# Planned issue and landing times of the small transfers of attention probabilities, in a kernel of attention and two MoE layers

## The chip, the core and the metric

The kernel runs on one core of a Trainium2 chip. The metric is device time in microseconds (us), the median of three runs. The engines named below are PE (TensorE, matrix products), DVE (VectorE), ACT (ScalarE), POOL (GpSimd) and SP (SyncE, which here issues nearly all DMA transfers, one after the other). Each engine takes its instructions in the order in which the program lists them.

## What is computed

Attention of 4 batches, 8 heads, 576 positions and 64 values per head, half of the heads with a local mask and half with a strided one; then a dense layer with squared ReLU; then a layer of 8 experts of which each token takes one.

```python
scores = scale * np.matmul(q, k.transpose(0, 1, 3, 2))
mask_local = (rel >= 0) & (rel < 32)
mask_strided = (rel >= 0) & (pos[None, :] % 32 == pos[:, None] % 32)
attn = softmax(np.where(masks, scores, -1e9))
x = np.matmul(attn, v)                      # to (2304 tokens, 512)
h = x @ w_in                                # 512 x 2048, the first layer
g = s * np.maximum(h, 0.0) ** 2 + b
x1 = g @ w_out                              # 2048 x 512, the second layer
out[mask_e] = gate * (np.maximum(x1[mask_e] @ w1[e], 0.0) @ w2[e])   # e of 8 experts
```

## The kernel before

The 2304 tokens are cut into five units (256, 512, 512, 512 and 512 tokens). Attention is cut into 23 groups, 0 to 22. The first nine take a transposing path on PE; groups 9 to 22 (the late groups, `attn_late`, line 780) are spread over the time in which PE does the dense layer of earlier units, and this is where the change lies.

The dense layer is a row of steps, one for each unit and each block of 128 hidden columns: `h` is computed by the first layer (line 1039, twelve matrix products of up to 512 columns), ACT and DVE make `g` of it (lines 987 to 1013), and the second layer (line 1073, again twelve) adds `g` times a weight block to four banks. A product of `float32r` halves is made of three passes, hence twelve.

A late group goes through these stages. Line 575 loads its queries and keys, and in another load its values. Line 800 makes the scores on PE into two banks. DVE adds the mask (line 815), takes maxima, subtracts, ACT takes the exponential (823), DVE sums and scales (825 to 830) and transposes blocks of 32 by 32 into `prt` (834). Line 842 moves the 32-row pieces of `prt` to their places in `phs`: eight small transfers of 32 KB for most groups, four for groups 13 and 18, all issued by SP. Line 857 then multiplies with the values on PE; this text calls it the product of the group. ACT and DVE split the result into a high and a low part in `xsl` (875, 879), which the first layer of the unit reads.

`prt`, `phs`, and the buffers of late queries/keys and of late values exist once each. So the transfers of a group wait for the product of the group before it, and so does the load of a group's values. The scores take a pair of banks, the product one bank of that pair.

The order of all this is not written by hand. `Order.run` (line 280) is a planner that runs while the program is built: each piece of work is a generator that yields `op((engine, duration), waits=...)`, and the planner always issues next what, by its own clocks, can start first. `("DMA", d)` occupies one clock of the planner's that stands for SP's queue, shared by all loads and transfers. `o.fin` is the planned end of the piece, `DMA_LAT` (1.8) what the planner adds until data have landed, and `t1` the planned landing of the small transfers: from then on the product may be placed (`ev`), and `prt` used again (`t_pt`). The durations in the planner do not bind the chip; they decide only in which order instructions stand on each engine.

Of the kernel before, what the change touches and what calls it, by code (L numbers as in the profile page):

```python
# [122 lines left out]
def span(g):  # L123
    kind, b, i0, n = GROUPS[g]
    if kind == "L":
        return b * S + i0 * QB, b * S + (i0 + n) * QB
    j0, j1, _ = part_of(g)
    return b * S + j0 * STRIDE, b * S + j1 * STRIDE
# [60 lines left out]
DMA_LAT = 1.8  # L189
# [114 lines left out]
def op(*engs, waits=(), dep=True, on=(), late=0.0):  # L304
    return engs, waits, dep, on, late
# [6 lines left out]
def body(ctx, tc, qkv, w12, moe_s, moe_b, wg, e12, out):  # L312
# [64 lines left out]
    o = Order()  # L377
# [68 lines left out]
    t_qe, t_qk, t_vv, t_pt, t_ph = Tok(NQE), Tok(1), Tok(1), Tok(1), Tok(1)  # L446
# [109 lines left out]
    for g, (kind, b, i0, n) in enumerate(GROUPS):  # L556
        t0, t1 = span(g)
# [23 lines left out]
    def attn(g):  # L581
        kind, b, i0, n = GROUPS[g]
        strided = kind == "P"
        if g >= NEARLY:
            yield from attn_late(g)
            return
# [193 lines left out]
    def attn_late(g):  # L780
# [51 lines left out]
        nb = 2 if w > QG else 1  # L832
# [1 line left out]
        nc.vector.transpose(out=prt[:, 0:nb * m * QG].rearrange("p (b c q) -> p b c q", b=nb, q=QG),  # L834
                            in_=pr[:, 0:m * 2 * QG].rearrange("p (c b q) -> p b c q", b=2, q=QG)[:, 0:nb])
        o.free(t_p)
        yield op(("DMA", 0.4 * nb), waits=[t_ph])
        for x in range(2):
            for y in range(nb):
                for p in range(2):  # L840
                    a, r = p * QB + x * QG, x * QB + y * QG
                    nc.sync.dma_start(out=phs[r:r + QG, p, x, 0:m * QG], in_=prt[a:a + QG, y * m * QG:(y + 1) * m * QG])
        t1 = o.fin + DMA_LAT
        o.free(t_pt, t1)
        ev = Ev()
        o.set(ev, t1)
# [1224 lines left out]
```

## Time and profile before

| what | value |
|---|---|
| median of 3 runs | 699.63 us (699.41 to 704.1) |
| the profiled execution, own time | 702.58 us |
| span of its first to last instruction | 700.8 us |
| PE busy | 674.9 us, 96% of the span |
| DVE busy | 345.7 us, 49% |
| ACT busy | 284.9 us, 41% |
| POOL busy | 39.5 us, 6% |
| share of 16 DMA engines' span taken by SP's queue | 29.4% |

A profile row names the line, the engine, the operation and the tiles (out<-in). In the timeline a row holds equal instructions that follow each other without a gap: start, length, count, and in brackets how long the engine had been idle before and what ended that. SPq is SP's queue: the time there is that of issuing, not of moving the data. Matrix products are pipelined, so a row's length ends after the start of the next one; the distance between the starts of two rows is what the first cost.

### The profile page before, as it was taken

The page shows a single profiled execution, that of the slowest core. Times are in us where ns is not written, and L with a number is a line of the kernel's source. Part 1 is how long each engine was busy: PE and PEld are TensorE (multiplying, and loading weights), DVE is VectorE, ACT ScalarE, POOL GpSimd, SP SyncE. Part 2 cuts the span into 40 slices and gives each one's busy share as a digit, 9 for nine tenths or more (in the row PEclk, how much of TensorE's full clock was granted, in tenths as well). Part 3 has the DMA queues.
Part 4 walks back from the last instruction along what each step waited for, and adds up shares of the span by engine and source line. Part 5 has one row for each costly group of instructions (what it writes and reads, how often), then busy time and mean ns, then how long its engine had stood idle before and what let it go on. Part 6 is the DMA issues. An engine that isn't in the chain of part 4 may idle for free. (4 is left out here: it accounts for less than half of the span.)

```text
span 700.8 us, 12794 instructions
## 1 busy us (share of the span) xinstructions
PE 674.9 (96%) x5028; PEld 568.6 (81%) x5028; DVE 345.7 (49%) x809; ACT 284.9 (41%) x598; POOL 39.5 (6%) x140
## 2 busy tenths in 40 slices
PE   8899999898998999999999999999999999999996
PEld 7788878797776778867877878888899899998896
DVE  6898886662253222134331134444567854764340
ACT  5777454454352233343333364554431432424221
POOL 7640000000000000000000000001000000000000
PEclk9999999999999999999999999999999999999999
DMA  8975156232323102031211023110120262307101
GB/s 314 406 272 173 55 172 215 69 117 81 115 98 118 58 24 65 1 134 52 72 36 46 1 90 121 61 61 31 61 91 1 71 230 99 121 1 256 64 12 63
DMA packets 31089, 72.32 MB, mean 103 GB/s; under 512 B 5806, under 2 KB 11695, under 8 KB 30259
## 3 DMA queue, kind: packets, MB, share of 16 engines
q1 hardware_dynamic: 30898, 71.46, 29.4%
q8 instruction: 40, 0.66, 0.4%
q14 instruction: 23, 0.18, 0.1%
q0 software_dynamic: 128, 0.02, 0.0%
HBM read 56.77 MB, written 11.69 MB: 98 GB/s over the span
## 5 line engine op out<-in xcount | busy, mean ns | idle before, releaser
L1039 PE MATMUL h<-xsl,w 128*128 128x512 f32 (+1 forms) x876 | 207.3, 382 | 0.0
L1073 PE MATMUL bk<-g,w 128*128 128x512 f32 (+1 forms) x864 | 198.8, 378 | 0.0
L1039 PEld LDWEIGHTS h<-xsl,w 128*128 128x128 f32 x876 | 157.2, 189 | 31.5 <-issue 0.8
L1073 PEld LDWEIGHTS bk<-g,w 128*128 128x128 f32 x864 | 155.4, 189 | 32.2 <-issue 1.3
L1013 DVE TENSOR_TENSOR g<-r,g 128x512 fp32r<-128x512 f32 (+1 forms) x73 | 48.1, 659 | 156.1 <-ACT g L1011 155.9
L987 ACT ACTIVATE r<-h 128x512 f32<-128x512 f32 (+1 forms) x80 | 44.4, 556 | 194.4 <-PE h L1039 190.6
L1544 PE MATMUL bk<-w,ht 128*128 128x512 f32 x384 | 96.8, 393 | 0.0
L1544 PEld LDWEIGHTS bk<-w,ht 128*128 128x128 f32 x384 | 68.6, 188 | 12.2
L1011 ACT ACTIVATE g<-r 128x512 fp32r<-128x512 f32 (+1 forms) x73 | 44.2, 605 | 2.7
L999 ACT ACTIVATE r<-r 128x512 f32<-128x512 f32 (+1 forms) x73 | 44.2, 606 | 2.2
L1437 ACT ACTIVATE ht<-h 128x256 fp32r<-128x256 f32 x24 | 9.2, 385 | 74.6 <-PE h L1598 54.8
L857 PE MATMUL bk<-phs,qkv 128*64 128x64 f32 (+2 forms) x408 | 17.9, 232 | 15.3 <-DMA phs<-prt 12.3
L857 PEld LDWEIGHTS bk<-phs,qkv 128*64 128x64 f32 x408 | 15.1, 143 | 21.4 <-issue 18.0
L1598 PEld LDWEIGHTS h<-x,wa 128*128 128x128 f32 x192 | 26.4, 188 | 2.4 <-issue 0.4
L1598 PE MATMUL h<-x,wa 128*128 128x256 f32 x192 | 28.0, 281 | 0.0
L1598 PE MATMUL bk<-x,wc 128*128 128x256 f32 x192 | 27.8, 280 | 0.0
L1598 PE MATMUL h<-x,wc 128*128 128x256 f32 x192 | 27.7, 280 | 0.0
L1598 PEld LDWEIGHTS h<-x,wc 128*128 128x128 f32 x192 | 25.6, 188 | 1.3 <-DVE su L1475 0.3
L879 DVE TENSOR_TENSOR xsl<-bk,xsl 128x512 fp32r<-128x512 f32 (+4 forms) x14 | 8.6, 613 | 35.5 <-ACT xsl L875 35.5
L875 ACT ACTIVATE xsl<-bk 128x512 fp32r<-128x512 f32 (+4 forms) x14 | 7.5, 535 | 43.1 <-PE bk L857 43.0
L1598 PEld LDWEIGHTS bk<-x,wc 128*128 128x128 f32 x192 | 24.8, 188 | 0.2 <-issue 0.2
L815 DVE TENSOR_TENSOR pr<-bk,ml 128x288 f32<-128x288 f32 (+5 forms) x17 | 7.6, 462 | 26.2 <-PE bk L800 26.2
(245 smaller groups left out, 748.1 us busy)
## 6 DMA issues: line engine op xcount, KB each, us to landing
raw<-w SPq DMA_DIRECT2D x32, 512.0 KB, 7.8
qkv<-qkv SPq DMA_DIRECT2D x14, 512.0 KB, 4.0
qkv<-qkv SPq DMA_DIRECT2D x8, 544.0 KB, 3.7
out<-ob SPq DMA_DIRECT2D x17, 256.0 KB, 3.2
xd<-x SPq DMA_DIRECT2D x4, 1024.0 KB, 3.8
wraw<-e SPq DMA_DIRECT2D x16, 256.0 KB, 2.7
xr<-xd SPq DMA_DIRECT2D x8, 512.0 KB, 5.2
X<-xd SPq DMA_DIRECT2D x4, 1024.0 KB, 10.1
```

What stands on the lines that cost most here:

```text
L815: nc.vector.tensor_tensor(out=ps4[:, :, i:j], in0=sc[:, :, i:j], in1=mask.unsqueeze(1).unsqueeze(1).to_broadcast([P, 2, j - i, w]), op=ALU ...
L857: nc.tensor.matmul(out=og[h * D:(h + 1) * D, p * tot + 2 * i * nq:p * tot + 2 * (i + 1) * nq], lhsT=vv[:, i, p, h, :], rhs=phs[:, p, :, c: ...
L879: nc.vector.tensor_sub(out=dst[1], in0=src, in1=dst[0].bitcast(F32))
L987: nc.scalar.activation(out=r, in_=h, func=AF.Relu)
L999: nc.scalar.activation(out=to, in_=r, func=AF.Square)
L1011: nc.scalar.activation(out=gt[:, 0, 0:U], in_=r, func=AF.Copy)
L1013: nc.vector.tensor_sub(out=gt[:, 1, 0:U], in0=r, in1=gt[:, 0, 0:U].bitcast(F32))
L1039: nc.tensor.matmul(out=h, lhsT=w_t[2 * fc][:, a, c * P:(c + 1) * P], rhs=xt(u, c, x), start=(c == 0 and n == 0), stop=(c == KD - 1 and n = ...
L1073: nc.tensor.matmul(out=acc[pu][c], lhsT=w_t[2 * pf + 1][:, a, c * P:(c + 1) * P], rhs=gt[:, x, 0:cols(pu)], start=(first and n == 0), stop ...
L1437: nc.scalar.activation(out=ht[:, 0, a:b], in_=src, func=AF.Relu)
L1544: nc.tensor.matmul(out=acc2[s, t][0], lhsT=box[k][:, x, t * P:(t + 1) * P], rhs=w_t["p", 2 * f + 1][:, a, :], start=(f == 0 and n == 0), s ...
L1598: nc.tensor.matmul(out=banks[to], lhsT=t[:, a, off + c * P:off + (c + 1) * P], rhs=x2[s, b][:, y, c, :], start=(first and c == 0 and n == ...
```

## The change

Two numbers in `attn_late` are changed: what the planner counts for issuing the small transfers, and what it adds until they have landed. `nb` is 2 for eight transfers and 1 for four.

```diff
-        yield op(("DMA", 0.4 * nb), waits=[t_ph])
+        yield op(("DMA", 2.55 * nb), waits=[t_ph])
         for x in range(2):
             for y in range(nb):
                 for p in range(2):
                     a, r = p * QB + x * QG, x * QB + y * QG
                     nc.sync.dma_start(out=phs[r:r + QG, p, x, 0:m * QG], in_=prt[a:a + QG, y * m * QG:(y + 1) * m * QG])
-        t1 = o.fin + DMA_LAT
+        t1 = o.fin + DMA_LAT + 0.4
```

For eight transfers the planner now counts 5.1 for the issue where it counted 0.8, and 2.2 until landing where it counted 1.8. No instruction is added or dropped on PE, SP and POOL; one eviction of 64 columns goes from ACT to DVE. What differs is the order.

On PE, in the middle of unit 3, the place of the product of group 20 (`bk_3659` before, `bk_3821` now), with the scores of group 21 (`bk_3795` before, `bk_3775` now). Before:

```order
L1039 MATMUL h<-xsl,w 128x512 x6
L857 MATMUL bk_3659<-phs,qkv 64x64 x16
L1039 MATMUL h<-xsl,w 128x512 x6
L1073 MATMUL bk_930<-g,w 128x512 x3
L1073 MATMUL bk_931<-g,w 128x512 x3
L1073 MATMUL bk_932<-g,w 128x512 x3
L1073 MATMUL bk_933<-g,w 128x512 x3
L1039 MATMUL h<-xsl,w 128x512 x6
L800 MATMUL bk_3795<-qkv 32x36 x32
L1039 MATMUL h<-xsl,w 128x512 x6
```

And now, from the same twelve matrix products of line 1039 on:

```order
L1039 MATMUL h<-xsl,w 128x512 x12
L1073 MATMUL bk_930<-g,w 128x512 x3
L1073 MATMUL bk_931<-g,w 128x512 x3
L1073 MATMUL bk_932<-g,w 128x512 x3
L1073 MATMUL bk_933<-g,w 128x512 x3
L1039 MATMUL h<-xsl,w 128x512 x6
L800 MATMUL bk_3775<-qkv 32x36 x32
L1039 MATMUL h<-xsl,w 128x512 x6
L857 MATMUL bk_3821<-phs,qkv 64x64 x16
```

The product moved behind 30 matrix products of the dense layer and behind the scores of group 21, which were after it.

On PE, in unit 2, the products of groups 14 and 15. Before, from the product of group 14 to that of group 15:

```order
L857 MATMUL bk_2684<-phs,qkv 64x64 x16
L1204 MATMUL bk_2683<-pick,lts 128x16 x4
L1073 MATMUL bk_932<-g,w 128x512 x3
L1073 MATMUL bk_933<-g,w 128x512 x3
L1039 MATMUL h<-xsl,w 128x512 x12
L1073 MATMUL bk_930<-g,w 128x512 x3
L1073 MATMUL bk_931<-g,w 128x512 x3
L1073 MATMUL bk_932<-g,w 128x512 x3
L1073 MATMUL bk_933<-g,w 128x512 x3
L857 MATMUL bk_2683<-phs,qkv 64x64 x16
```

And now, again from the product of group 14 (`bk_2694`) to that of group 15 (`bk_2695`):

```order
L857 MATMUL bk_2694<-phs,qkv 64x64 x16
L1073 MATMUL bk_930<-g,w 128x512 x3
L1073 MATMUL bk_931<-g,w 128x512 x3
L1073 MATMUL bk_932<-g,w 128x512 x3
L1073 MATMUL bk_933<-g,w 128x512 x3
L1039 MATMUL h<-xsl,w 128x512 x12
L1073 MATMUL bk_930<-g,w 128x512 x3
L1073 MATMUL bk_931<-g,w 128x512 x3
L1073 MATMUL bk_932<-g,w 128x512 x3
L1073 MATMUL bk_933<-g,w 128x512 x3
L857 MATMUL bk_2695<-phs,qkv 64x64 x16
```

Both products moved back, and 36 matrix products of the dense layer stand between them where 30 and the small products of line 1204 stood.

On SP, at the same place: `xd_76` is the store of unit 1's result; then come the small transfers of groups 14 and 15, and loads of line 575. The first two loads of 1024 columns are the values of groups 15 and 16, the two of 1032 the queries and keys of groups 16 and 17. Before:

```order
L1169 DMA xd_76<-x_2457 128x2048
L842 DMA phs<-prt 32x256 x8
L575 DMA qkv<-qkv 128x1024
L575 DMA qkv<-qkv 128x1032
L842 DMA phs<-prt 32x256 x8
L575 DMA qkv<-qkv 128x1024
L575 DMA qkv<-qkv 128x1032
L842 DMA phs<-prt 32x256 x8
```

And now:

```order
L1169 DMA xd_76<-x_2468 128x2048
L842 DMA phs<-prt 32x256 x16
L575 DMA qkv<-qkv 128x1024
L575 DMA qkv<-qkv 128x1032
L575 DMA qkv<-qkv 128x1024
L575 DMA qkv<-qkv 128x1032
L842 DMA phs<-prt 32x256 x8
```

The eight transfers of group 15 moved ahead of the values of group 15, directly behind those of group 14.

## Rows read from the trace of the kernel before

**Rows 1.** Busy time by engine in two stretches: from:to length, then busy us (instructions) per engine, PEclk, DMA share, GB/s.

```profile
90.00:130.00 40.00, 38.68 (x348) 31.25 (x346) 31.05 (x63) 17.94 (x33) 0.13 (x2) 1.00 0.51 166
...
380.00:700.00 320.00, 315.27 (x1864) 274.03 (x1863) 154.16 (x413) 114.89 (x214) 5.09 (x16) 1.00 0.23 79
```

**Rows 2.** Waits of PE: engine, line waited for: us in total, times, longest.

```profile
PE bk L857 <- DMA phs<-prt: 12.3, 17, 2.2
...
PE bk L857 <- DMA qkv<-qkv: 2.3, 1, 2.3
...
PE bk L857 <- DVE w L910: 0.3, 1, 0.3
PE bk L857 <- issue: 0.2, 1, 0.2
```

**Rows 3.** Timeline of PE, products of groups 9, 11, 12, 13 and 15.

```profile
96.53 0.76 PE L800 MATMUL bk<-qkv 64*32 64x36 f32 x64
97.23 1.67 PE L1039 MATMUL h<-xsl,w 128*128 128x512 f32 x6
99.23 0.34 PE L857 MATMUL bk<-phs,qkv 128*64 128x64 f32 x4 [0.33 <-DVE w L910]
...
131.25 2.29 PE L857 MATMUL bk<-phs,qkv 128*64 128x48 f32 x32 [1.98 <-DMA phs<-prt]
...
160.32 1.15 PE L857 MATMUL bk<-phs,qkv 128*64 128x64 f32 x32
...
166.81 0.69 PE L857 MATMUL bk<-phs,qkv 128*64 128x64 f32 x16 [2.30 <-DMA qkv<-qkv]
...
218.39 0.34 PE L857 MATMUL bk<-phs,qkv 128*64 128x64 f32 x4 [2.16 <-DMA phs<-prt]
219.02 1.04 PE L857 MATMUL bk<-phs,qkv 128*64 128x64 f32 x28 [0.29 <-DMA phs<-prt]
219.98 4.61 PE L1039 MATMUL h<-xsl,w 128*128 128x512 f32 x12
```

**Rows 4.** Timeline of SP's queue, small transfers and the loads behind them.

```profile
105.67 4.95 SPq L842 DMA_DIRECT2D phs<-prt  x8
...
161.38 2.41 SPq L842 DMA_DIRECT2D phs<-prt  x4
163.83 4.02 SPq L575 DMA_DIRECT2D qkv<-qkv  x3
...
212.58 4.94 SPq L842 DMA_DIRECT2D phs<-prt  x8
```

**Rows 5.** All small transfers of line 842: ns of one min/median/max, and issue to landing.

```profile
L842 SPq DMA_DIRECT2D phs<-prt x104: 507/588/1377, 93.4 to 371.4; - x104
...
DMA to landing us min/median/max: 1.7/1.8/3.8
```

**Rows 6.** Timeline of PE, twelve matrix products of 512 and of 256 columns.

```profile
142.43 1.62 PE L1073 MATMUL bk<-g,w 128*128 128x258 f32 x12
143.88 1.59 PE L1039 MATMUL h<-xsl,w 128*128 128x256 f32 x12
...
344.20 2.88 PE L1039 MATMUL h<-xsl,w 128*128 128x512 f32 x12
346.92 2.88 PE L1073 MATMUL bk<-g,w 128*128 128x512 f32 x12
```

**Rows 7.** DMA issues: loads of line 575, count, KB each, us to landing (208.2:214, then whole span).

```profile
qkv<-qkv SPq DMA_DIRECT2D x1, 512.0 KB, 3.5
...
qkv<-qkv SPq DMA_DIRECT2D x4, 384.0 KB, 9.8
```

**Rows 8.** Busy time as in rows 1, behind the waits of groups 11 and 15.

```profile
131.30:134.70 3.40, 3.27 (x35) 2.86 (x36) 0.95 (x3) 1.01 (x2) 0.00 (x0) 0.50 0.06 11
...
220.00:223.50 3.50, 3.50 (x10) 2.74 (x9) 0.69 (x1) 0.60 (x1) 0.00 (x0) 0.51 0.47 154
```

**Rows 9.** Timeline of DVE, the mask of group 21.

```profile
340.06 0.46 DVE L815 TENSOR_TENSOR pr<-bk,ml 128x288 f32<-128x288 f32 x1 [2.12 <-PE bk L800]
```

## The prediction

> **What bounds the kernel now.** I read the busy time by stretch first. After 380 us PE works 315 of 320 us [rows 1], so nothing but PE's own work counts there, and that work is the same before and after. What can be won lies earlier, in PE's waits. The list of PE's waits puts nearly all that happen after the start at one line, the product of the late groups: 12.3 us in 17 waits for the small transfers, 2.3 us once for a load of values, and 0.3 and 0.2 us beside them, together 15.1 us [rows 2]. The timeline shows how one looks: PE comes to the product of group 15, stands 2.16 us until seven of the eight transfers have landed, does a few products, and stands another 0.29 us for the eighth [rows 3]. The 0.3 us put down to a weight (group 9) fit the seventh transfer as well, since the product reads no weight. Ten of the fourteen late groups wait for small transfers, for 0.4 to 2.45 us each.
>
> The reason is in SP's timeline and in the rows of line 842: one small transfer takes 0.588 us to issue, and 1.8 us from issue to landing, so eight take 4.94 us to issue [rows 4, 5]. From 212.58, the first issue of group 15, to 219.02, when PE goes on with the last piece, is 6.44 us [rows 3, 4]. The planner counted 0.8 + 1.8 = 2.6 us and so placed the product some 4 us too early. It now counts 5.1 + 2.2 = 7.3, about 0.9 us more than the trace.
>
> A second cost follows two of the waits. After the waits of groups 11 and 15 (1.98 and 2.16 us) the granted clock is 0.50 and 0.51 for about 3.4 us [rows 8], that is 1.2 instead of 2.4 GHz. Twelve matrix products then take 4.61 us where they take 2.88 [rows 3, 6], so each stretch costs 1.7 us. The wait of 2.30 us of group 13 has no such stretch behind it in this execution, so it does not come with every wait of this length.
>
> **The change, part by part.** *Products placed later.* Twelve matrix products of 512 columns cost 2.72 us (346.92 less 344.20 [rows 6]), one 0.227 us. In the new order the product of group 20 stands behind 30 more of them and behind the scores of group 21 (0.70 us, 97.23 less 96.53 [rows 3]): 6.8 + 0.7 = 7.5 us later in PE's work. Counted in the same way, the ten groups that wait move by 4.1 us (18 products: groups 9, 17, 21) to 10.3 us (group 16). The longest wait of the ten is 2.45 us, so all would be covered, if the transfers don't slide along. They mostly don't: a group's transfers follow from its scores, whose places move by no more than 1.5 us but for group 16, and from `phs` being free, that is from the product before. Gain: 12.3 + 0.3 + 0.2 = 12.8 us.
>
> *Group 13.* Its wait is for its values, which SP issues behind four small transfers that wait for the product of group 12: 160.32, 161.38, 163.83, and data at 166.81 [rows 3, 4]. Neither product 12 nor this order on SP moves. The product of group 13 moves behind 6 products of 512 columns (1.36 us) and 6 of 258 (0.7 us, half of 143.88 less 142.43 [rows 6]), 2.1 us. Of 2.3 us 0.2 remain.
>
> *Group 15, where a new wait begins.* SP now issues the transfers of group 15 directly behind those of group 14, ahead of the values of group 15. `phs` exists once, so they wait for the product of group 14, and so do the values behind them in the queue. With E as the end of that product, the eight issues run from E to E + 5.0, and the values are issued then and land 3.5 us later (the load of exactly these values [rows 7]): E + 8.5. PE has 36 products until the product of group 15, 8.2 us. A wait of about 0.4 us takes the place of 2.45. From both sides: nothing if they land in 3.0, as the values of group 13 did from issue to use (163.83 to 166.81 [rows 3, 4]), 6.7 us if in 9.8, the slowest of these loads [rows 7]. I take 3.5, because the row is this very load in its old place, a few us away. The Trainium skill, "DMA: Bandwidth & Descriptors", section "Anatomy of one DMA", puts a transfer at a fixed 2.0 us plus its bytes at 436 GB/s; an estimate from that page is 3.2 us for 512 KB, and by it the wait would be 0.1 and the sum 0.3 us better. The trace's 3.5 decides.
>
> *Loads of weights* (line 894) and the store and fetch of partial sums change places with loads of values on SP. The store of unit 1 goes ahead of two loads that only later groups need. The five loads of weights around groups 10 and 11 keep their number between the two sets of transfers. DVE, which has to split them, is busy 31.05 of 40 us there [rows 1], and still waits for PE at nearby places. I cost this at nothing; the cover is DVE's lead, which shows in that PE's waits hold no more than 0.3 us that could be a weight's [rows 2]. If the lead went, every us beyond it would be PE's.
>
> *Product behind the next group's scores.* In groups 10, 11, 16 and 20 the scores of the next group now go ahead of the product, and take both banks of the pair; the product needs one back, which DVE frees after adding the mask. DVE stands idle before that addition (2.12 us for group 21), starts when the scores end and takes 0.46 us [rows 9]. PE has six products in between, 1.36 us. Nothing on the path, with 0.8 us in hand.
>
> *Evictions, and the starts of units.* The products' evictions come later too; by the order, more than 70 products of the dense layer (16 us at 0.227) stand between the last product of a unit and the first layer that reads it, so a move of 2 to 7 us is covered.
>
> **The sum.** Waits 15.1, less 0.2 (group 13) and 0.4 (group 15): 14.5 us. Half-clock stretches: 2 x 1.7 = 3.4 us. Against the profiled execution's own 702.58: 702.58 - 17.9 = 684.7 us. That execution is 2.95 us above the median of 699.63. What it has more is not shown; stretches of half clock that other executions don't have could be part of it. So for the median I count one of the two: 699.63 - 14.5 - 1.7 = **683.4 us**. With both it is 681.7, with none 685.1.
>
> **The rivals.** *Part of the waits comes back* (one buffer for `phs`, one for the values: what a later product holds up comes late to the next). At group 15 with a load of 7.8 to 9.8 us instead of 3.5: 4.3 to 6.3 us more, and a half-clock stretch, 1.7: 689 to 691. For it: the queue order is new there, and the loads at the kernel's start do take so long [rows 7]. Against it: this very load took 3.5 us a few us from there [rows 7]. If the values of group 13 were as slow as well (9.8 against 3.0), another 6.8 + 1.7: about 700, no change.
>
> *The change does nothing:* each group's transfers slide as far as its product, since each waits for the product before it. Then PE waits as now, 699.6. Against it: by the trace the issue starts with the transposition, not with the product before, in all groups but 13; after the change only group 15's begins at that product.
>
> *Slower:* the products of groups 10, 11, 16 and 20 wait for the next group's scores. If the bank came free not with the mask but only when that group's probabilities are transposed (scores at 96.53, first transfer at 105.67: 9.1 us [rows 3, 4]), PE, which by the order gets there 2.1, 2.7, 4.8 and 2.1 us after the scores (1.36 us for six products, 0.70 for the scores), would wait 7.0 + 6.4 + 4.3 + 7.0 = 24.7 us and fall to half clock four times (7 us): 683.4 + 31.7 = 715. It decides from about 4 us per place (4 x 4 = 16, the gain). Against it: group 9 already has this order, and its product started at 99.23, 6.4 us before the transfers of group 10 [rows 3, 4].
>
> **How the numbers follow.** The forecast, 681 to 687 us, gets 0.72. Waits coming back in part, around 690, 0.14; these still lie below 692.6, the bound for faster by over 1%. Waits back in full, by slow loads or by sliding transfers, around 699.6, 0.10. Slower, 0.04. 1% is about what a measurement of this kernel tells from no change. So faster 0.86, same 0.10, slower 0.04. The range is 680.5 to 689.5: below it takes in both half-clock stretches and no wait left (681.1), above the near end of the partial case.
>
> **What would show it.** Right: the waits of line 857 for `phs` fall from 17 to at most two or three and under 1 us; groups 13 and 15 show a few tenths for `qkv`; the granted clock is 1.00 from 20 us to the end of the dense layer; PE's busy time is down by only some 3 us, the span by 17 to 18. Wrong: a wait of line 857 over 2 us for `qkv` at group 15 (slow load), one put down to DVE's line 815 (bank), PE waits at line 1039 for `w` (weights pushed back), or waits for `phs` that remain in the groups of unit 4.

## The result

| | before | after |
|---|---|---|
| median | 701.01 us (699.41 to 704.1, 4 runs) | 682.69 us (682.05 to 683.02, 4 runs) |
| ratio | | 0.9732, 95% interval 0.9693 to 0.9772 |
| profiled execution: span | 700.8 us | 681.3 us |
| PE busy | 674.9 us, 96% | 671.0 us, 98% |

683.4 was forecast, with a range of 680.5 to 689.5. The median before is 1.4 us above the one shown at first, since a fourth run joined it; more on that below.

The list of PE's waits after the change, in the columns of [rows 2], is short:

```profile
PE bk L619 <- DMA qkv<-qkv: 1.1, 2, 0.8
PE bk L857 <- DMA qkv<-qkv: 1.0, 2, 0.7
```

No product waits for small transfers any more (12.3 us in 17 waits in [rows 2]), and what is left at line 857 are the two waits for values that were expected. The timeline of PE shows where the products of groups 11, 13, 14 and 15 stand now:

```profile
134.32 1.14 PE L857 MATMUL bk<-phs,qkv 128*64 128x48 f32 x32
...
161.77 0.71 PE L857 MATMUL bk<-phs,qkv 128*64 128x64 f32 x16 [0.31 <-DMA qkv<-qkv]
...
204.27 1.15 PE L857 MATMUL bk<-phs,qkv 128*64 128x64 f32 x32
205.35 3.02 PE L1073 MATMUL bk<-g,w 128*128 128x512 f32 x12
208.21 2.88 PE L1039 MATMUL h<-xsl,w 128*128 128x512 f32 x12
210.93 2.88 PE L1073 MATMUL bk<-g,w 128*128 128x512 f32 x12
214.49 1.27 PE L857 MATMUL bk<-phs,qkv 128*64 128x64 f32 x32 [0.68 <-DMA qkv<-qkv]
```

Where [rows 3] show a first part of a product, a gap, and the rest, there is one row of 32 now: even the gap for the eighth transfer is gone. Group 11 has no bracket (1.98 us before) and takes 1.14 us instead of 2.29, because the clock is up. Busy time by engine, in the columns of [rows 1], shows a granted clock of 1.00 over the whole of the stretch that had the two halves of [rows 8], and PE busy for all but 1.8 us of it:

```profile
20.00:380.00 360.00, 358.17 (x3014) 294.35 (x3004) 181.06 (x374) 164.53 (x347) 21.24 (x75) 1.00 0.33 113
```

So of the 19.5 us between the two spans 14.1 us are waits at line 857 (15.1 to 1.0), and 3.9 us are PE's busy time (674.9 less 671.0), of which the two stretches of half clock account for an estimated 3.4. The rest is not the change's: some 2 us less at the kernel's start, where line 619 waits for the first loads, and 0.9 us more between PE's last product and the end. The wait at the start in the first profile of before was:

```profile
PE bk L619 <- DMA qkv<-qkv: 3.4, 4, 1.2
```

and it is 1.1 us here; in the profiles of the experiments it was found anywhere between 0.5 and 2.8 us.

### The profile page after: what moved, and what is told of

Read it like the earlier page. It is cut to its first block, busy times and chain, and to the rows that moved or that the text cites. A ratio compares the mean times of both kernels' runs of the same rounds, so it can differ in the third digit from the quotient of the medians.

```text
span 681.3 us, 12800 instructions
## 1 busy us (share of the span) xinstructions
PE 671.0 (98%) x5028; PEld 567.2 (83%) x5028; DVE 344.6 (51%) x810; ACT 284.2 (42%) x597; POOL 39.4 (6%) x140
## 5 line engine op out<-in xcount | busy, mean ns | idle before, releaser
L1039 PE MATMUL h<-xsl,w 128*128 128x512 f32 (+1 forms) x876 | 203.6, 380 | 0.0
L1502 ACT ACTIVATE ob<-bk,scl 128x512 f32<-128x512 f32 x16 | 11.0, 690 | 22.1 <-PE bk L1544 21.4
L543 POOL TENSOR_SCALAR_AFFINE_SELECT ml<-ml 32x36 f32<-32x36 f32 (+1 forms) x52 | 19.8, 381 | 3.3
L1478 DVE TENSOR_TENSOR dd<-h,su 128x256 f32<-128x256 f32 x16 | 6.8, 423 | 24.1 <-PE h L1598 24.1
```

The costliest lines, as they stand in the source:

```text
L543: nc.gpsimd.affine_select(out=x, in_=x, pattern=pattern, compare_op=ALU.is_ge, fill=NEG, base=base, channel_multiplier=sign)
L1039: nc.tensor.matmul(out=h, lhsT=w_t[2 * fc][:, a, c * P:(c + 1) * P], rhs=xt(u, c, x), start=(c == 0 and n == 0), stop=(c == KD - 1 and n = ...
L1502: nc.scalar.activation(out=ob, in_=src, func=AF.Copy, scale=scl[:, i:i + 1])
```

## The experiments

The theory: PE gains what its products no longer wait, because they stand behind more of PE's other work when the small transfers land. The main rival: the gain comes from the order itself, of loads on SP or of work on the engines. A second question was which of the two numbers does it, and how exact they have to be. All medians of before on the chips of these runs lie between 700.5 and 702.3 us.

**Same order, faster transfers.** The order of the kernel before, but in groups 14 to 22 POOL, idle there, issues half of the small transfers.

```diff
-                    nc.sync.dma_start(out=phs[...], in_=prt[...])
+                    (nc.gpsimd if p and g >= 14 else nc.sync).dma_start(out=phs[...], in_=prt[...])
```

> The order of the kernel before on PE, DVE and ACT, to the row; for groups 14 to 22 half of the small transfers are issued by POOL, the other half by SP. Theory (PE waits because eight issues of 0.588 us stand one behind the other): with four on each queue the last lands about 4.2 us after the first issue instead of 6.4, if POOL issues as fast as SP; the waits of groups 14 to 22, 10.3 us, fall under 1 us and the time by 8 to 12, to 688 to 692. If POOL takes a microsecond each, the waits stay. Rival (the gain of the change is one of order, not of when the data land): no change.

693.45 us, ratio 0.9864 (0.9832 to 0.9895), 8.8 us less than the median of before. POOL issues one in 0.496 us, as the row of line 842 among the groups of instructions by line has it (least, median and most ns):

```profile
L842 POOL DMA_DIRECT2D phs<-prt x34: 496/496/729, 198.4 to 358.1; - x34
```

PE's waits for small transfers:

```profile
PE bk L857 <- DMA phs<-prt: 3.9, 5, 2.0
```

And PE's timeline at group 19:

```profile
301.73 1.27 PE L857 MATMUL bk<-phs,qkv 128*64 128x64 f32 x32 [1.10 <-DMA phs<-prt]
```

Of the five waits for `phs` three belong to groups 9 and 11, which were left alone; of the rest 0.34 us are left at group 15 and 1.10 at group 19. The waits of groups 14 to 22 fell from 10.3 to 1.4 us, not to under 1 as forecast, and the time lies 1.5 us above the range, on a chip whose median before is 702.27. That the 8.9 us of waits and the 8.8 us between the medians agree so closely is partly chance: in this profile one stretch of half clock is left where the first of before had two, the start is 2.5 us shorter, and the end after PE's last product 3.2 us longer. No instruction of PE, DVE or ACT changed its place. So the time was lost where the small transfers land after PE has come, and the rival that only the order matters falls.

**Both numbers, one at a time.** First the issue time on SP's clock alone, with the landing planned as before:

```diff
-        yield op(("DMA", 0.4 * nb), waits=[t_ph])
+        yield op(("DMA", 2.55 * nb), waits=[t_ph])
-        t1 = o.fin + DMA_LAT
+        t1 = o.fin + DMA_LAT - 2.15 * nb
```

> Only the issue time counted (2.55 per four transfers) on the planner's clock of SP; the landing is planned as in the kernel before. The products move by 2.1 to 3.8 us, since their values are planned later, and SP keeps the values of group 15 ahead of its small transfers. Theory: every wait of 0.4 to 2.45 us is covered but 0.2 of group 13: 682 to 684, no wait for values at group 15. Rival (the product has to be planned behind the measured landing, 6.4 us): about half of the gain, 690.

682.45 us, ratio 0.9707 (0.968 to 0.9734): the whole gain. PE's waits at line 857 in its profile:

```profile
PE bk L857 <- DMA phs<-prt: 1.5, 1, 1.5
...
PE bk L857 <- DMA qkv<-qkv: 0.3, 1, 0.3
```

The wait for values at group 15 is gone, as expected, since SP issues these values ahead of the small transfers here. A wait of 1.5 us at group 10 was not expected. Its small transfers took 7.20 us to issue, where eight took 4.95 in [rows 4]. SP's own waits show why: before the seventh it stood until the load of weights issued eight transfers earlier had landed, and before the eighth until the load of queries and keys behind that one had. SP's timeline, its waits from 100 to 114 us, and the landing of the weights:

```profile
104.86 7.20 SPq L842 DMA_DIRECT2D phs<-prt  x8
...
SPq L842 <- DMA raw<-w: 1.2, 1, 1.2
SPq L842 <- DMA qkv<-qkv: 0.6, 1, 0.6
...
raw<-w SPq DMA_DIRECT2D x1, 512.0 KB, 8.1
```

Moves of 2.1 to 3.8 us were enough for the rest.

Then the landing alone, 2.15 per four transfers and 0.4 later, with the issue counted as before:

```diff
-        t1 = o.fin + DMA_LAT
+        t1 = o.fin + DMA_LAT + 0.4 + 2.15 * nb
```

> Only the landing is planned late (by 2.15 per four transfers and 0.4), the issue counted on SP's clock as before. The order on SP in the stretch of the late groups and the places of thirteen of fourteen products are those of the change; group 16 moves by 4.1 us instead of 10.3. Theory: the same as the change, 682 to 684, with the same waits for values at groups 13 and 15. Rival (the count on SP's clock does it): 690 or more.

688.46 us, ratio 0.9831 (0.9802 to 0.986): 6 us short of the change. Both theory and rival missed: products wait no more than in the change, and yet a new wait came, at the scores of group 16. PE's timeline from the product of group 14 on:

```profile
204.61 1.15 PE L857 MATMUL bk<-phs,qkv 128*64 128x64 f32 x32
205.69 3.02 PE L1073 MATMUL bk<-g,w 128*128 128x512 f32 x12
208.54 2.88 PE L1039 MATMUL h<-xsl,w 128*128 128x512 f32 x12
216.09 0.90 PE L800 MATMUL bk<-qkv 64*32 64x36 f32 x64 [4.66 <-DMA qkv<-qkv]
```

SP's timeline there, and the load that PE waited for:

```profile
193.39 17.24 SPq L842 DMA_DIRECT2D phs<-prt  x16
210.68 10.93 SPq L575 DMA_DIRECT2D qkv<-qkv  x4
```

Busy time by engine after the wait:

```profile
216.10:219.40 3.30, 3.30 (x70) 2.56 (x70) 2.30 (x5) 0.45 (x1) 0.00 (x0) 0.51 0.02 5
```

On SP the queries and keys of group 16 stand behind the eight transfers of group 15, which wait for the product of group 14 and take 5 us to issue. The planner, which counted 0.8 us for them, thought the load early and put the scores 24 products behind that product; they wait 4.66 us and half a clock follows. In the change the scores stand behind 48 products and the product of group 15, and don't wait. So the issue time on SP's clock places more than the products: every load behind the small transfers, and what needs it, is placed by it too.

**How exact the numbers have to be.** Three sizes beside the change's own. The 0.4 us of landing alone:

```diff
-        t1 = o.fin + DMA_LAT
+        t1 = o.fin + DMA_LAT + 0.4
```

> Only the 0.4 us added to the planned landing; the issue still counted at 0.4 per four transfers. In the new order only the products of groups 11, 15 and 16 move, by 1.3 to 1.4 us. Theory (a wait shrinks by what its product moves on PE): group 11 from 1.98 to 0.6, group 15 from 2.45 to about 1.0, group 16 from 0.41 to 0, all others unchanged: 3.1 us of waits less, and no half-clock stretch, up to 3.4 us: 693 to 697. Rival (the order of loads on SP makes the gain, which hardly differs here): no change, 699 to 702.

698.46 us, ratio 0.9941 (0.9918 to 0.9964): 2.5 to 5.8 us less than before. The time lies above the range forecast, but the median before is 702.27 on this chip; the fall of 3.8 us is near the low end of the 3.1 to 6.5 that were expected. The products of groups 11, 15 and 16 in its timeline:

```profile
130.67 0.32 PE L857 MATMUL bk<-phs,qkv 128*64 128x48 f32 x4 [0.58 <-DMA phs<-prt]
...
216.70 0.34 PE L857 MATMUL bk<-phs,qkv 128*64 128x64 f32 x4 [0.79 <-DMA phs<-prt]
...
232.37 0.33 PE L857 MATMUL bk<-phs,qkv 128*64 128x56 f32 x4 [0.59 <-DMA phs<-prt]
```

Groups 11 and 15 lost 1.4 us each of their first wait, exactly the move. Group 16 won nothing, because its scores moved along with the product; I had looked at the product alone. Its two waits even grew from 0.41 to 0.84 us, and group 11 now stands another 0.27 for its eighth transfer, so that the waits of line 857 fell by 1.9 us in all and not by 3.1. Nor did every half-clock stretch go: one follows the wait of 2.43 us for the values of group 13, which had none behind it in the first profile of before. Busy time by engine there:

```profile
164.50:168.00 3.50, 3.50 (x13) 3.04 (x12) 0.70 (x2) 1.31 (x3) 0.00 (x0) 0.51 0.52 150
```

About half of the true issue time:

```diff
-        yield op(("DMA", 0.4 * nb), waits=[t_ph])
+        yield op(("DMA", 1.2 * nb), waits=[t_ph])
```

> Issue counted at 1.2 per four transfers (2.4 for eight, half of the true 4.94), landing at 1.8 as before. The products move by 1.3 to 3.4 us. Theory (what counts is the product's move in whole pieces of the dense layer, 1.36 us each, against its wait): left are about 0.9 us at group 13 and 0.2 at groups 19 and 22, in all about 1.3: 683 to 684.5, as good as the full count. Rival (gain in proportion to the number): half of it, 690 to 692.

685.55 us, ratio 0.9784 (0.9756 to 0.9812): about four fifths of the gain for half of the number, not in proportion to it. 1 us more than forecast is a wait at group 15, whose eighth transfer, issued at 210.22, landed only 3.5 us later (PE's timeline, then that issue with its us to landing):

```profile
212.49 0.34 PE L857 MATMUL bk<-phs,qkv 128*64 128x64 f32 x4
214.00 1.03 PE L857 MATMUL bk<-phs,qkv 128*64 128x64 f32 x28 [1.17 <-DMA phs<-prt]
...
phs<-prt SPq DMA_DIRECT2D x1, 32.0 KB, 3.5
```

The median is 1.8 and the longest 3.8 in [rows 5]. The two loads ahead of these transfers had landed 3 us before this one was issued, so they don't explain it; the cause stays open.

Twice the true issue time:

```diff
-        yield op(("DMA", 0.4 * nb), waits=[t_ph])
+        yield op(("DMA", 5.1 * nb), waits=[t_ph])
-        t1 = o.fin + DMA_LAT
+        t1 = o.fin + DMA_LAT + 0.4
```

> Issue counted at 5.1 per four transfers, twice the true one. The products move by 9 to 27 us, those of groups 13 and 18 up to the start of the unit that reads them, and the planner fills its own idle time on PE with 50 products without use. Theory: no wait for small transfers, but 50 x 0.11 = 5.5 us of filling and waits of the first layer at two or three unit starts, 1 to 2 us each: 688 to 693, slower than the change. Rival (later is always at least as good): 682 to 684.

688.33 us, ratio 0.9826 (0.9792 to 0.986): slower than the change by some 6 us, in the range expected, but in part for another reason. No product waits, and neither does the first layer at the start of a unit, where waits had been expected. The timeline of PE shows what it costs, first at a wait for queries and keys of group 12, then at the start of unit 2:

```profile
136.83 0.85 PE L800 MATMUL bk<-qkv 64*32 64x64 f32 x64 [2.27 <-DMA qkv<-qkv]
...
181.39 4.83 PE L1957 MATMUL bk<-xsl 128*128 128x256 f32 x39
186.28 0.69 PE L857 MATMUL bk<-phs,qkv 128*64 128x64 f32 x16
186.90 0.98 PE L1957 MATMUL bk<-xsl 128*128 128x256 f32 x6
```

The product of group 13 has moved up to the unit that needs it, and the planner filled the time that it believed idle with products without use (line 1957): 45 of the 50 stand here and take 5.7 us (181.39 to 186.28 and 186.90 to 187.71). "Later" is safe only as long as the unit's start is far.

**Values first.** The change, with the loads of late groups preferred to the small transfers when both become possible together:

```diff
-P_QKL = 0.1
+P_QKL = -0.2
```

> The change, and the loads of late queries, keys and values preferred to the small transfers where both become possible at one time (priority -0.2 for 0.1). SP now issues the values of groups 13 and 15 ahead of their small transfers. Theory (the two waits left, 0.31 and 0.68 us, come from the queue order): both vanish and no new one comes, 1.0 us less than the change: 681.7. Rival (the small transfers behind a 512 KB load land late): waits for phs at groups 13 or 15, 683 to 685.

681.14 us, ratio 0.9697 (0.9674 to 0.9719). The waits at groups 13 and 15 are gone; no product of any group waits. SP's timeline at group 13 shows two loads ahead of the small transfers, which [rows 4] show behind them:

```profile
156.34 0.81 SPq L575 DMA_DIRECT2D qkv<-qkv  x2
157.25 2.41 SPq L842 DMA_DIRECT2D phs<-prt  x4
```

It was then run again beside the change, on one chip:

> The changed kernel again, beside the next one on the same chip. Theory: 682.7 within a few tenths; waits at groups 13 and 15 for values, 0.3 and 0.7 us, as in its first profile, since they come from the order on SP; the waits at the kernel's start (line 619) differ from run to run by a microsecond or two.

> The change with the values preferred, again, beside the change on the same chip. Theory (only the two waits of groups 13 and 15 go): 1.0 us below the change, 681.7. Rival (the 1.5 us seen between the two on different chips was the chip or the start): no difference beyond the interval.

The change took 681.79 us (681.23 to 682.53), 0.9 below what was expected from its first runs; with values first 681.19 (680.61 to 682.02). The ratios to before are 0.9718 and 0.9706, with intervals that overlap. PE's waits in the second profile of the change are:

```profile
PE bk L857 <- DMA qkv<-qkv: 0.7, 2, 0.4
```

0.6 us between the medians is what these 0.7 us would give, but six runs each don't set it apart from nothing. That the two waits come from the order on SP is shown by the profiles; that the time falls with them is not.

**The kernel before, once more**, for the spread between its executions:

> The kernel before, profiled once more. Theory: the waits of line 857 come again at the same groups with the same lengths within 0.1 us, 15 us in all, since they follow from the order; what differs between its executions (699 to 704) lies in the number of half-clock stretches, 0 to 3 of 3.4 us each, and in the waits at the start. Rival: the waits themselves differ by several us.

702.07 us. PE's waits at line 857:

```profile
PE bk L857 <- DMA phs<-prt: 12.5, 17, 2.3
PE bk L857 <- DMA qkv<-qkv: 2.9, 1, 2.9
```

Busy time by engine after the wait of group 15:

```profile
219.50:223.00 3.50, 3.50 (x24) 2.81 (x20) 0.69 (x1) 0.60 (x1) 0.00 (x0) 0.53 0.44 152
```

Seventeen waits for 12.5 us again; only the one for values differs (2.9 for 2.3). This time a stretch of half clock follows group 15 but not group 11, and one of twice the length lies at the start, from 14.7 to 21.7 us. Over eleven runs of before on one chip the time goes with the mean granted clock:

| mean granted clock of the run | times of before, us |
|---|---|
| 1.000 | 698.38, 699.26 |
| 0.995 to 0.997 | 700.64, 700.75, 701.25, 701.47 |
| 0.990 to 0.993 | 702.30, 703.51, 703.56, 703.83, 705.58 |

One stretch of 3.4 us at half clock lowers the mean by 0.0024 (3.4 x 0.5 / 700), but the mean alone doesn't count those that cost time: in every profile of this case the clock is also low at the very end, when PE has done its last product. Busy time by engine at the end of the first profile of before, and at the start of this one:

```profile
697.90:700.75 2.85, 0.00 (x0) 0.00 (x0) 0.00 (x0) 0.00 (x0) 0.00 (x0) 0.51 0.01 4
...
14.70:21.70 7.00, 6.87 (x97) 6.08 (x91) 6.20 (x13) 5.27 (x26) 2.77 (x9) 0.51 1.04 412
```

So the 0.993 of the first profile are the stretches of groups 11 and 15 and the end, and the 0.991 of this one are the stretch of group 15, the one at the start and the end. How many stretches a run without a profile had isn't shown; the table fits more of them in the longer runs. The six runs of the change beside them have 0.997 to 0.999 and spread over 1.3 us instead of 7.2.

## Why the prediction was right

*Products placed later.* Right, and closely: 12.8 us of waits for small transfers were to go, and 12.8 went. That the transfers would not slide along held in all groups that had waited for them; the same order with faster transfers gave the same kind of gain, so it is the meeting of PE and data that counts.

*Group 13.* 0.2 us were to remain, 0.31 and 0.22 did in two profiles.

*Group 15.* The mechanism was right, its two terms were a little off. The product of group 14 ends at 205.35, and SP is through with the eight issues 5.0 us later, as forecast:

```profile
193.08 17.22 SPq L842 DMA_DIRECT2D phs<-prt  x16
210.34 9.43 SPq L575 DMA_DIRECT2D qkv<-qkv  x4
```

The values landed 3.9 us after issue and were used after 4.15 (210.34 to 214.49), where I took 3.5 from the old place of this load; PE needed 8.5 us for its 36 products, where I took 8.2. The wait was 0.68 instead of 0.4 (5.0 + 3.5 - 8.2 is 0.3, strictly), and 0.45 in the second profile. The landing, as the list of DMA issues has it:

```profile
qkv<-qkv SPq DMA_DIRECT2D x1, 512.0 KB, 3.9
```

The estimate from the Trainium skill, "DMA: Bandwidth & Descriptors", "Anatomy of one DMA", was 3.2 us for that load, further off than the row's 3.5. The section gives its figures for transfers that GpSimd issues; SP issued this one.

*Loads of weights, the product behind the next group's scores, evictions and unit starts* were costed at nothing. No wait of PE at any of these places appears in the profile after, among them groups 10, 11, 16 and 20, on which the slower rival rested. What would happen if the unit starts came near is shown by the doubled number.

*Half clock.* Both stretches went. For the median I counted one, 1.7 us, since I did not know what the profiled execution had more than the median. The runs of before show in part what it is: stretches differ from one execution to the next (two in one profile, one and a longer one at the start in the other), and so do the waits at the start; its medians lie some 2 to 3 us above the two runs whose mean clock is 1.000. How many stretches the median execution held isn't shown, so the one that I counted is neither borne out nor refuted, and that 683.4 came within 0.7 of the measured 682.69 is partly luck: the fall from before was 18.3 us where 16.2 were forecast, and 1.4 us of that difference are the median before, which three runs had put lower than four did.

*The rivals.* Waits that come back in part had a chance of 0.14, mainly for slow loads at group 15. They did not come in the change, but the experiment on the landing alone shows one of that kind, a few rows further on: 4.66 us for queries and keys behind the same small transfers, plus 1.7 us of half clock. I had weighed only the values there.

## What to carry to other kernels

When an order is planned, count a transfer as what its queue is held for and as what passes until data land, both from the trace: eight small transfers cost 4.9 us of SP's queue, six times what was planned, and everything behind them was placed by that number. Exactness mattered little: half of the true number brought about four fifths of the gain, since work moves in whole pieces and the waits were short, while twice the number cost some 6 us, as results then came up to where they were needed. And where a transfer waits for a buffer, look at every load behind it in the queue, not only at the one that its own consumer needs.

## What the runs showed of the hardware

A wait of PE may or may not be followed by a stretch of about 3.4 us at the lower of its two clock levels. In the first profile of before it came after waits of 1.98 and 2.16 us and not after 2.30; in the second after 2.25 and not after 2.95 or 2.00; with 0.4 us of landing alone after 2.43; with two queues after 1.10 us at group 19 and not after 1.99 and 2.25. The rows of group 19, from just after that wait:

```profile
301.70:304.10 2.40, 2.37 (x41) 2.33 (x42) 0.01 (x1) 0.60 (x1) 0.00 (x0) 1.00 0.08 12
304.10:307.50 3.40, 3.40 (x9) 2.65 (x9) 2.50 (x9) 0.97 (x2) 0.00 (x0) 0.51 0.47 151
```

The clock still is 1.00 for 2.4 us after the wait and falls only then. The kernel before, with nearly the same waits at line 857 in both of its profiles, took 698 to 706 us, and with these waits most of the spread went too.

POOL issued a small transfer in 0.496 us against 0.588 on SP. With both queues at once SP took 3.20 us for its four transfers at group 19, 0.8 more than the 2.41 in [rows 4]. That isn't the second queue's doing: with SP alone its eight took 5.76 us there, 0.8 more than 4.95, too. In both traces they stand directly behind the store of a unit's result (line 1169); at groups 15, 16, 17, 20, 21 and 22 SP's four took 2.41 to 2.44 us beside POOL's. SP's timeline at group 19 with two queues, and before:

```profile
295.07 0.33 SPq L1169 DMA_DIRECT2D xd<-x  x1
295.84 3.20 SPq L842 DMA_DIRECT2D phs<-prt  x4
...
304.00 0.33 SPq L1169 DMA_DIRECT2D xd<-x  x1
304.42 5.76 SPq L842 DMA_DIRECT2D phs<-prt  x8
```
